# Two attention blocks on one core: the value sums of two groups of heads in one phase, and one buffer laid into another

## The chip, the cores and the metric

The kernel runs on one core of a Trainium2 chip. Its engines work side by side: TensorE (PE in the profile, with PEld for the loading of weights into its array), VectorE (DVE), ScalarE (ACT), GpSimd (POOL), and SyncE (SP), which here only issues DMAs. The metric is the time of one execution on the device in microseconds (us); smaller is better.

## The reference

Two independent blocks A and B, each with an input x of 2048 rows by 640, weights wqkv (640 x 1920) and wo (640 x 640), and 32 heads of 20 columns. Their outputs stand side by side in an output of 2048 x 1280.

```
A:  q, k, v = heads of x @ wqkv
    p = softmax(q k^T / sqrt(20)) over the keys 0 <= row - key < 256
    out = (p v) @ wo
B:  q, k, v = heads of x @ wqkv;  phi(t) = (t + 1 if t > 0 else exp(t)) + 1e-6
    kv = phi(k)^T v;  z = sum of phi(k);  o = phi(q) kv / (phi(q) z + 1e-6)
    out = o @ wo
```

## The kernel before

The rows are worked in 4 blocks s of 512. A's 32 heads are 8 groups g of 4 heads. All instructions of all engines are written in one order, and each engine works its own in that order; semaphores make one engine wait for another.

**Score tiles.** `scores` (L775) makes one tile: up to four heads' score products on PE into the only `S_ps` (4 of the 8 PSUM banks), one exponential on ACT of 128 x 2048 values into a buffer `p` (L805), and masks on POOL (`affine_select`, L826). There are 76 score tiles, numbered here 0 to 75: 16 in the first block, 20 in each other. `tiles_of` (L39) lists them: from the second block on, two groups g and h = g + 1 share five tiles. Tile 2 of the five completes nothing, tile 3 completes g, tile 5 completes h. Tiles 2 and 3 hold a middle part whose masks are larger (a 128 x 512 select and two of 128 x 1024 each); tiles 1, 4 and 5 have two selects of 128 x 512. In the first block two groups share four tiles, and the second and the fourth complete one each.

**Value sums.** `values` (L837) multiplies the p of one group with v: 56 matmuls (40 in the first block) that each use 32 columns of the array, four side by side, into one bank `dense`. For the group h its own order is: the middle part of tile 3, the parts of tile 4, the parts of tile 5. DVE then transposes the bank into `T` (L866, one buffer), and a deferred `rest` divides by the softmax sums (L877, L883). A group's sums are issued two tiles after the tile that completes it, straight behind that tile's score products.

**Fill.** All other PE work is fill: the projections of A and B, B's sums over keys, the output projections. It uses full 128 x 128 weights, and a chain of matmuls per bank (`dense`, 4 banks, shared with the value sums). A list `plan` gives every bank of fill a time in units of tiles, and other work (loads, DMA moves, selects) too; sorted by time it is one sequence. After each tile's products and value sums, `take` (L1101) issues fill until the tile's credit of matmul columns is used: `rate` columns per tile, less `VALUES` for each value sum. PSUM banks are copied out by ACT or DVE, whichever the counters of `evac` (L266) find less loaded; banks of phi take an exponential on ACT and two DVE operations (L301, L304), which are deferred in `later` until the next `flush`.

**Parts that the change touches.** A's v projection of a block (`a_v`, L469) reads v's weights `w_sb["A"]`; the last block's has plan times 43 to 49, its q 36 to 41.5 and its k 41 to 46. `kv_T` (L524) holds B's kv in blocks of 120 columns with zeros between; GpSimd clears it at the start (L525), `b_kv` (L640) has DVE copy the products into it (L656, L663), `own_heads` (L621) masks them with two POOL selects, and `b_merge` (L666) multiplies them with wo. `zk` is masked by two small POOL selects (L224). q's and k's rows for the groups 5 to 7 are moved by 4 DMA writes and 4 DMA reads through DRAM (`moves`, L379).

```
        if ready and ready[0][0] + LAG <= i:
            ...
            _, at = ready.popleft()
            values(*at, held.pop(at))
            ...
            credit -= VALUES
```

Of the kernel before, what the change touches and what calls it, by code (L numbers as in the profile page):

```python
# [9 lines left out]
P = 128  # L10
# [3 lines left out]
BF16 = mybir.dt.bfloat16  # L14
# [5 lines left out]
NG = H // 4  # L20
# [3 lines left out]
FILL = 386520  # L24
TAIL = 13000

VALUES = 2200
TILE = 3000
COPY = 160
AHEAD = 600  # L30
# [72 lines left out]
def kernel(  # L103
# [10 lines left out]
    nc = tc.nc  # L114
    _, S, D = A_x.shape
    KT = D // P
    NS = S // SB
# [7 lines left out]
    def pool(name, bufs, space=None):  # L125
        if space is None:
            return ctx.enter_context(tc.tile_pool(name=name, bufs=bufs))
        return ctx.enter_context(tc.tile_pool(name=name, bufs=bufs, space=space))

    wp = pool("weights", 1)  # L130
# [1 line left out]
    qp = pool("q", 2)  # L132
    kp = pool("k", 3)
    vp = pool("v", 3)
    pp = pool("p", 5)
    pqp = pool("pq", 2)
    op1 = pool("o1", 2)
    pl_ = pool("plow", 2)
# [11 lines left out]
    w_sb = {}  # L150
# [87 lines left out]
    def flush(before=None):  # L238

        while later and (before is None or later[0][0] <= before):  # L240
            later.pop(0)[1]()
# [90 lines left out]
    for c in range(KT):  # L332
        m = EXTRA * c
        while m < EXTRA * (c + 1):
            n = min(EXTRA * (c + 1) - m, DH - m % DH)
# [184 lines left out]
    GD = GH * DH  # L520
    NGR = KT + 1
    PAD = GD
    G = w_sb["B"][:, :, D : 2 * D]
    kv_T = wp.tile([P, NGR, PAD + GD + 8 * KT], BF16, name="kv_T")  # L524
    nc.gpsimd.memset(kv_T[:], 0.0)  # L525
    kv_own = kv_T[0:GD, :, PAD : PAD + GD]

    pk_of = {}
# [104 lines left out]
    def kv_ready(step):  # L633

        if step == 0:
            keep_own_head(zk[:], 0, NHC, 1)
        else:
            own_heads(3 - 2 * step)

    def b_kv():  # L640

        for gs in (range(0, 4), range(4, NGR)):
            ps = bank()
            for i, g in enumerate(gs):
                w = min(GD, D - g * GD)
                for kt in range(KT):
                    nc.tensor.matmul(  # L647
                        ps[0:w, i * GD : i * GD + w],
                        lhsT=w_sb["B"][:, kt, 2 * D + g * GD : 2 * D + g * GD + w],
                        rhs=G[:, kt, g * GD : g * GD + w],  # L650
                        start=(kt == 0),
                        stop=(kt == KT - 1),
                    )
                yield KT * GD
            full = [g for g in gs if (g + 1) * GD <= D]
            nc.vector.tensor_copy(  # L656
                out=kv_own[:, full[0] : full[-1] + 1, :],
                in_=ps[0:GD, 0 : len(full) * GD].rearrange("p (g d) -> p g d", d=GD),
            )
            if len(full) < len(gs):  # L660
                w = D - KT * GD
                at = len(full) * GD
                nc.vector.tensor_copy(out=kv_own[0:w, KT, 0:w], in_=ps[0:w, at : at + w])  # L663
            yield End(0)
# [107 lines left out]
    def key(s, rel):  # L772
        return 4 * s + rel
# [63 lines left out]
    def values(s, g, held):  # L837


        O_ps = dps.tile([P, SB], F32, name="dense")  # L840
        todo = []
        for (_, rel, q0, n, col, step), (p, low) in held:
            if rel == "M":
                own = key(s, q0 // P)
                todo.append((own, low, q0, n, col - LOW, step, columns))
                if own >= 2:
                    todo.append((own - 2, p, q0 + HALF, n, col, step, columns_p))
            else:
                todo.append((key(s, rel), p, q0, n, col, step, columns_p))
        for i, (kb, p, q0, n, col, step, of) in enumerate(todo):  # L850
            at = (kb % TPS * H + 4 * g) * HV
            for j in range(4):
                nc.tensor.matmul(  # L853
                    O_ps[32 * j : 32 * (j + 1), q0 : q0 + n],
                    lhsT=v_flat[kb // TPS % 3][:, at + j * HV : at + j * HV + 32],
                    rhs=of(p, j, col, n, step),
                    start=(i == 0),
                    stop=(i == len(todo) - 1),
                    tile_position=(0, 32 * j),
                    skip_group_check=True,  # L860
                )
        if turns[0] and g == 0:
            settle()

        T = tp.tile([P, SB // 32, 32], F32, name="T")
        nc.vector.transpose(out=T.rearrange("p b e -> p (b e)"), in_=O_ps[:])  # L866
        add_load(d=1500)
        if s not in norm_A:
            norm_A[s] = (
                np_.tile([P, SB // 32, P], BF16, name="N"),  # L870
                np_.tile([P, SB // 32, 32], BF16, name="Nr"),
            )
        N, Nr = norm_A[s]

        def rest():
            r = sp.tile([P, SB // 32, 1], F32, name="recA")
            nc.vector.reciprocal(out=r[:], in_=T[:, :, DH:HV])  # L877
            lo = g * DH
            for dst, a, b in ((N, lo, min(lo + DH, P)), (Nr, max(lo, P), lo + DH)):
                if a >= b:  # L880
                    continue
                at = a - P if dst is Nr else a
                nc.vector.tensor_tensor(  # L883
                    out=dst[:, :, at : at + b - a],
                    in0=T[:, :, a - lo : b - lo],
                    in1=r[:].to_broadcast([P, SB // 32, b - a]),
                    op=ALU.mult,
                )
            if lo < P <= lo + DH:
                oT_A[s] = op1.tile([P, KT, SB], BF16, name="oT")  # L890

                def turn(j):
                    quadrant = slice(32 * j, 32 * (j + 1))
                    nc.sync.dma_start_transpose(
                        out=oT_A[s][:, j, :].rearrange("p (b e) -> p b e", e=32),
                        in_=N[quadrant].rearrange("p b x -> p (b x)"),
                    )
                    turns[0] -= 1

                if s < NS - 1:  # L900
                    turns[0] = 4
                    for j in range(4):
                        soon(lambda j=j: turn(j), 2 + 2 * j)
            if g == NG - 1:
                nc.vector.transpose(
                    out=oT_A[s][:, KT - 1, :], in_=Nr.rearrange("p b e -> p (b e)")
                )

        later.append((begun[0], rest))
# [123 lines left out]
    def at(t0, t1, gen, n):  # L1033
        for i in range(n):
            plan.append((t0 + (i + 0.5) / n * (t1 - t0), gen, i == n - 1))

    def do(t0, t1, fns):
        fns = list(fns)
        for i, fn in enumerate(fns):
            plan.append((t0 + (i + 0.5) / len(fns) * (t1 - t0), None, fn))  # L1040
# [12 lines left out]
        at(t - 0.5, t + 3.5, first_rows[n], c)  # L1053
        reads_of(t + 5, t + 6, n, 0)
    for s, tq, tk, tv in ((1, (2.2, 8), (7, 12), (10, 15)), (2, (19, 26), (25, 32), (16, 22)),
                          (3, (36, 41.5), (41, 46), (43, 49))):
        at(*tq, a_rows("q", s), KT)
        reads_of(tq[1] + 1.5, tq[1] + 3.5, "q", s)
        at(*tk, a_rows("k", s), KT)
        reads_of(tk[1] + 1.5, tk[1] + 3.5, "k", s)  # L1060
        at(*tv, a_v(s), 2 * TPS)
# [4 lines left out]
    for s, t in ((0, 6), (1, 11), (2, 24.2), (3, 28.2)):  # L1066
        do(t, t, [lambda s=s: load_tok(s)])
    do(40.5, 40.5, [lambda: kv_ready(0)])
    at(42, 43.4, b_kv(), 2)
    do(44, 45.4, [lambda c=c: kv_ready(c) for c in (1, 2)])  # L1070
    for s, tq, td, tx in ((0, (39.5, 45), 46.3, 46.8), (1, (45, 50), 53, 54.3),
# [36 lines left out]
        return done  # L1108

    units = [u for s in range(NS) for u in tiles_of(s)]  # L1110
    LAG = 2
    held, ready = {}, deque()
    n_values = NS * NG
    rate = (FILL - TAIL + n_values * VALUES) / len(units)
    credit = 0.0
    for i, (s, parts, selects, done) in enumerate(units):
        p = scores(s, parts, selects)
        flush()
        credit += rate
        for part in parts:  # L1120
            held.setdefault((s, part[0]), []).append((part, p))
        if done is not None:
            ready.append((i, (s, done)))
        if ready and ready[0][0] + LAG <= i:
            last = i == len(units) - 1
            if last:
                credit -= take(2000)
            _, at = ready.popleft()
            values(*at, held.pop(at))
            if last:  # L1130
                flush()
            credit -= VALUES
            if len(quotients_due) > 2 or i > URGENT:
                quotient()
        else:
            quotient()
        credit -= take(credit)
        pass_tile()
    while ready:
        take(5500)  # L1140
        _, at = ready.popleft()
        values(*at, held.pop(at))
        flush()
    turn_last(NS - 1)
    for _ in fill:
        pass
# [31 lines left out]
```

## Time and profile before

| | |
|---|---|
| time, median of 3 runs | 255.71 us (255.31 to 256.76) |
| time of the profiled execution | 256.37 us |
| its span | 254.6 us |
| PE busy | 244.4 us |
| ACT, DVE, POOL busy | 199.2, 181.6, 170.7 us |
| stretch 180.6 to 238.1 us (last block's tiles): ACT, DVE, POOL busy of 57.5 us | 51.5, 50.0, 43.2 us |
| granted TensorE clock | 1.00 |

The span is the time from the first to the last instruction of the program; 1.77 us of the profiled execution lie around it. PE matmuls are pipelined: a row's length holds the latency of its last matmul, so the distance from one start to the next tells what a matmul costs, and the row's length does not. A row of the timeline that ends in [x <- y] had its engine idle for x us before it, and y is what ended the wait.

### The profile page before, as it was taken

What the parts mean: (1) busy time and instruction counts of PE and PEld (TensorE: products, weight loads), DVE (VectorE), ACT (ScalarE), POOL (GpSimd) and SP (SyncE); (2) the same over time, 40 slices, a digit from 0 to 9 for tenths busy, and PEclk for the clock granted to TensorE, in tenths of its full rate; (3) what the DMA queues carried; (4) which work ended last, traced back from release to release, by engine and by line L of the source; (5) the groups of instructions that cost most, each with busy time, mean ns of one, the idle gap of its engine ahead of it and who ended that gap; (6) DMA issues with size and microseconds to landing.
All of it is one profiled execution on the core that took longest, in us unless ns stands there. A gap on an engine that the chain in (4) does not pass through costs nothing.

```text
span 254.6 us, 10488 instructions
## 1 busy us (share of the span) xinstructions
PE 244.4 (96%) x4578; PEld 142.9 (56%) x4625; DVE 181.6 (71%) x315; ACT 199.2 (78%) x261; POOL 170.7 (67%) x214
## 2 busy tenths in 40 slices
PE   8999999999999999999999999999999999999995
PEld 7644446557755455466445555556555565655573
DVE  0445797697854578777665877688879889979652
ACT  3566879889768797997668788899988999998442
POOL 7115788778784957658495867959676695987700
PEclk9999999999999999999999999999999999999999
DMA  6996588798660342995468395525769987584714
GB/s 215 311 219 194 109 194 130 189 263 156 96 96 3 90 147 36 240 273 149 83 127 170 87 207 103 145 43 78 199 83 180 178 98 151 97 177 81 234 45 164
DMA packets 68371, 37.16 MB, mean 146 GB/s; under 512 B 51557, under 2 KB 67301, under 8 KB 68325
## 3 DMA queue, kind: packets, MB, share of 16 engines
q1 hardware_dynamic: 68325, 36.49, 66.2%
q8 instruction: 36, 0.59, 1.0%
q14 instruction: 10, 0.08, 0.1%
HBM read 14.42 MB, written 9.83 MB: 95 GB/s over the span
## 4 chain that ended last, share of the span: by engine, by line
PE 90%; issue 4%; DVE 4%; ACT 1%; ACTq 0%
PE dense L287 48%; PE S_ps L785 11%; PE dense L853 9%; PE dense L564 9%; PE dense L422 9%; PE dense L207 1%; DVE phi L304 1%; PE dense L718 1%; ACT e L297 1%; PE dense L188 1%; PE dense L675 1%; PE dense L647 1%; DVE tok L754 1%; DVE e L301 1%; ACT osb L272 0%
## 5 line engine op out<-in xcount | busy, mean ns | idle before, releaser
L805 ACT ACTIVATE p<-S_ps 128x2048 bf16<-128x2048 f32 x76 | 142.1, 1870 | 31.0 <-PE S_ps L785 30.4
L826 POOL TENSOR_SCALAR_AFFINE_SELECT p<-p 128x512 bf16<-128x512 bf16 (+1 forms) x152 | 121.7, 823 | 62.6 <-ACT p L805 60.3
L287 PE MATMUL dense<-xA,wqk 128*128 128x512 bf16 x188 | 48.9, 380 | 1.3 <-issue 0.8
L826 POOL TENSOR_SCALAR_AFFINE_SELECT plow<-p 128x1024 bf16<-128x1024 bf16 x32 | 40.4, 1261 | 0.0
L785 PEld LDWEIGHTS <-kpad 20*128 20x128 bf16 (+1 forms) x1664 | 20.0, 97 | 27.9 <-issue 26.5
L785 PE MATMUL S_ps<-qpad,kpad 20*128 20x64 bf16 (+3 forms) x1664 | 34.6, 211 | 1.0 <-issue 0.4
L866 DVE STREAM_TRANSPOSE T<-dense 128x512 f32<-128x512 f32 x32 | 22.7, 710 | 15.7 <-PE dense L853 15.3
L301 DVE TENSOR_SCALAR e<-e 128x512 bf16<-128x512 bf16 x40 | 23.6, 590 | 13.2 <-ACT e L297 13.0
L287 PEld LDWEIGHTS <-wqk 128*128 128x128 bf16 x200 | 17.9, 98 | 20.6 <-issue 2.3
L304 DVE SCALAR_TENSOR_TENSOR phi<-dense,e 128x512 bf16<-128x512 f32 x40 | 27.7, 691 | 1.6
L422 PE MATMUL dense<-wA,xA 128*128 128x320 bf16 x160 | 26.5, 303 | 0.2 <-issue 0.2
L853 PE MATMUL dense<-p,vA 128*32 128x64 bf16 (+2 forms) x1152 | 26.1, 222 | 0.1
L287 PE MATMUL dense<-wB,xB 128*128 128x512 bf16 (+1 forms) x156 | 25.3, 297 | 0.4 <-issue 0.3
L297 ACT ACTIVATE e<-dense 128x512 bf16<-128x512 f32 x40 | 23.4, 592 | 2.5 <-PE dense L287 1.9
L287 PE MATMUL dense<-wo,oT 128*128 128x128 bf16 (+2 forms) x155 | 24.5, 297 | 0.5 <-issue 0.2
L287 PE MATMUL dense<-xB,wB 128*128 128x512 bf16 x90 | 24.4, 380 | 0.5 <-issue 0.3
L564 PE MATMUL dense<-tok,phi 128*128 128x129 bf16 (+1 forms) x152 | 23.9, 296 | 0.9 <-issue 0.8
L287 PE MATMUL dense<-wB,xA 128*128 128x128 bf16 (+1 forms) x152 | 22.8, 295 | 0.7 <-issue 0.5
L853 PEld LDWEIGHTS <-vA 128*32 128x32 bf16 x1664 | 21.5, 96 | 3.3 <-issue 0.8
L883 DVE TENSOR_TENSOR N<-T,recA 128x320 bf16<-128x320 f32 (+1 forms) x28 | 19.6, 698 | 2.7 <-DMA oT<-N 1.8
L272 ACT ACTIVATE osb<-dense 128x512 bf16<-128x512 f32 (+1 forms) x26 | 14.6, 571 | 7.6 <-PE dense L287 7.1
L422 PEld LDWEIGHTS <-xA 128*128 128x128 bf16 x160 | 15.2, 99 | 8.0 <-issue 0.4
(66 smaller groups left out, 241.6 us busy)
## 6 DMA issues: line engine op xcount, KB each, us to landing
out_dram<-osb SPq DMA_DIRECT2D x7, 640.0 KB
x_scr<-xB SPq DMA_DIRECT2D x4, 640.0 KB
tok<-in_B_x_dram SPq DMA_DIRECT2D x4, 640.0 KB
xB<-x_scr SPq DMA_DIRECT2D x4, 640.0 KB
wB<-in_B_wqkv_dram SPq DMA_DIRECT2D x3, 800.0 KB
q_scr<-qpad SPq DMA_DIRECT2D x16, 60.0 KB
k_scr<-kpad SPq DMA_DIRECT2D x16, 60.0 KB
qpad<-q_scr SPq DMA_DIRECT2D x16, 60.0 KB
```

The costliest lines, as they stand in the source:

```text
L287: nc.tensor.matmul(dst, lhsT=lhs(kt), rhs=rhs(kt), start=(kt == 0), stop=(kt == KT - 1))
L297: nc.scalar.activation(out=view(e), in_=src, func=ACT.Exp)
L301: nc.vector.tensor_scalar(out=e[:], in0=e[:], scalar1=1e-6, scalar2=1.0 + 1e-6, op0=ALU.add, op1=ALU.min)
L304: nc.vector.scalar_tensor_tensor(out=dst, in0=src, scalar=0.0, in1=view(e), op0=ALU.max, op1=ALU.add)
L422: nc.tensor.matmul(ps[:, 0 : hh * DH], lhsT=xt[:, kt, tb * P : (tb + 1) * P], rhs=w_sb["A"][:, kt, i * hh * DH : (i + 1) * hh * DH], start ...
L564: nc.tensor.matmul(out, lhsT=pk[:, tb, c * P : (c + 1) * P], rhs=x[:, tb, lo:hi], start=(i == 0), stop=(i == len(blocks) - 1),)
L785: nc.tensor.matmul(columns(S_ps[0:keys], j, col, n, step), lhsT=kt[32 * j : 32 * j + DH, g, ko : ko + keys], rhs=q_pad[s][32 * j : 32 * j ...
L805: nc.scalar.activation(out=p.rearrange("p a j q -> p j a q"), in_=S_ps.rearrange("p j (a q) -> p j a q", a=2), func=ACT.Exp, scale=scale,)
L826: nc.gpsimd.affine_select(out=dst, in_=src, pattern=[[0, 4], [0, n // HALF], [sgn, HALF]], compare_op=ALU.is_ge, fill=0.0, base=base, chan ...
L853: nc.tensor.matmul(O_ps[32 * j : 32 * (j + 1), q0 : q0 + n], lhsT=v_flat[kb // TPS % 3][:, at + j * HV : at + j * HV + 32], rhs=of(p, j, c ...
L866: nc.vector.transpose(out=T.rearrange("p b e -> p (b e)"), in_=O_ps[:])
L883: nc.vector.tensor_tensor(out=dst[:, :, at : at + b - a], in0=T[:, :, a - lo : b - lo], in1=r[:].to_broadcast([P, SB // 32, b - a]), op=AL ...
```

## The change

- From now on the sums of both groups of a pair are issued in one phase, `values` twice in a row, g first. From the second block on this is one tile after tile 5 (before: g in tile 5 and h two tiles after tile 5). In the first block it is two tiles after the fourth tile. The last two groups of the last block stay as they were. Between the two, the first group's `rest` is flushed.
- `VALUES` goes from 2200 to 1500 columns, so that `rate` goes from 5841 to 5546 columns per tile.
- There are six p buffers, not five.
- `kv_T` is no tile of its own any more. It is the first 1680 columns of v's weights of A, and so it can be cleared only when A's last v projection is done: the clearing moves from the start to plan time 41, behind `zk`'s selects at 40.5.
- A's last v projection moves from 43..49 to 35.8..40.6, q from 36..41.5 to 38.5..44.5 and k from 41..46 to 43..48. Their DMA moves follow.

```
-VALUES = 2200
+VALUES = 1500
...
-    pp = pool("p", 5)
+    pp = pool("p", 6)
...
-    kv_T = wp.tile([P, NGR, PAD + GD + 8 * KT], BF16, name="kv_T")
-    nc.gpsimd.memset(kv_T[:], 0.0)
+
+    KVW = PAD + GD + 8 * KT
+    kv_T = w_sb["A"].rearrange("p k n -> p (k n)")[:, 0 : NGR * KVW].rearrange(
+        "p (g w) -> p g w", w=KVW
+    )
...
-                          (3, (36, 41.5), (41, 46), (43, 49))):
+                          (3, (38.5, 44.5), (43, 48), (35.8, 40.6))):
...
     do(40.5, 40.5, [lambda: kv_ready(0)])
+    do(41, 41, [lambda: nc.gpsimd.memset(kv_T, 0.0)])
     at(42, 43.4, b_kv(), 2)
...
-        if done is not None:
-            ready.append((i, (s, done)))
-        if ready and ready[0][0] + LAG <= i:
+
+        single = (s, done) in ((NS - 1, NG - 2), (NS - 1, NG - 1))
+        if done is not None and (done % 2 or single):
+            lag = 1 if s and not single else 2
+            ready.append((i + lag, s, (done,) if single else (done - 1, done)))
+        if ready and ready[0][0] <= i:
             last = i == len(units) - 1
             if last:
                 credit -= take(2000)
-            _, at = ready.popleft()
-            values(*at, held.pop(at))
-            if last:
-                flush()
-            credit -= VALUES
+            _, sv, groups = ready.popleft()
+            for g in groups:
+                values(sv, g, held.pop((sv, g)))
+                if last or g != groups[-1]:
+                    flush()
+                credit -= VALUES
             if len(quotients_due) > 2 or i > URGENT:
                 quotient()
         else:
...
     while ready:
         take(5500)
-        _, at = ready.popleft()
-        values(*at, held.pop(at))
-        flush()
+        _, sv, groups = ready.popleft()
+        for g in groups:
+            values(sv, g, held.pop((sv, g)))
+            flush()
```

## The prediction

> **What bounds the kernel now.** I read the page first: busy shares, the slices, the chain that ended last.
>
> ```profile
> PE 244.4 (96%) x4578; PEld 142.9 (56%) x4625; DVE 181.6 (71%) x315; ACT 199.2 (78%) x261; POOL 170.7 (67%) x214
> PE   8999999999999999999999999999999999999995
> PE 90%; issue 4%; DVE 4%; ACT 1%; ACTq 0%
> ```
>
> PE is full in every slice and carries the chain, so time goes only where PE is given less, or made to wait. The waits of PE in the list of waits are small (2.1 us on "issue" is the largest), so I next looked at what PE pays for a phase of value sums. The timeline of PE over tile 32, which has one, and tile 33, which has none:
>
> ```profile
> 109.57 0.55 PE L785 MATMUL S_ps<-qpad,kpad 20*128 20x192 bf16 x40
> 110.04 0.21 PE L853 MATMUL dense<-plow,vA 128*32 128x64 bf16 x4
> ...
> 110.26 0.66 PE L853 MATMUL dense<-p,vA 128*32 128x64 bf16 x28
> 110.84 1.25 PE L287 MATMUL dense<-wB,xB 128*128 128x512 bf16 x4
> ...
> 112.46 0.54 PE L785 MATMUL S_ps<-qpad,kpad 20*128 20x64 bf16 x40
> 112.94 0.60 PE L287 MATMUL dense<-xA,wqk 128*128 128x512 bf16 x2
> ```
>
> By the starts, scores and sums take 110.84 - 109.57 = 1.27 us and the same scores alone 0.48: the phase costs 0.79. Then POOL, because the change lets a pair's second sums follow their masks by one tile where there were two, and puts work into POOL's queue. Its timeline at tiles 42 to 46, the groups of kv's selects and clearing, and a late stretch:
>
> ```profile
> 141.21 0.69 POOL L826 TENSOR_SCALAR_AFFINE_SELECT p<-p 128x512 bf16<-128x512 bf16 x1 [0.39 <-ACT p L805]
> 141.85 1.39 POOL L826 TENSOR_SCALAR_AFFINE_SELECT plow<-p 128x1024 bf16<-128x1024 bf16 x1
> 143.31 1.15 POOL L826 TENSOR_SCALAR_AFFINE_SELECT p<-p 128x1024 bf16<-128x1024 bf16 x1
> 144.93 0.67 POOL L826 TENSOR_SCALAR_AFFINE_SELECT p<-p 128x512 bf16<-128x512 bf16 x1 [0.46 <-ACT p L805]
> ...
> 150.76 1.57 POOL L826 TENSOR_SCALAR_AFFINE_SELECT p<-p 128x512 bf16<-128x512 bf16 x2 [1.55 <-ACT p L805]
> ```
> ```profile
> L623 POOL TENSOR_SCALAR_AFFINE_SELECT kv_T<-kv_T 120x720 bf16<-120x720 bf16 x2 | 2.2, 1083 | 0.0
> L525 POOL MEMSET kv_T<- 128x1680 bf16 x1 | 1.5, 1497 | 0.0
> L224 POOL TENSOR_SCALAR_AFFINE_SELECT zk<-zk 128x40 bf16<-128x40 bf16 x2 | 1.1, 531 | 0.1
> ```
> ```profile
> 222.01 4.66 POOL L826 TENSOR_SCALAR_AFFINE_SELECT p<-p 128x1024 bf16<-128x1024 bf16 x5
> ```
>
> The reader is to see that POOL waits for ACT before tiles 42, 43 and 45: it has slack, but a tile of the large masks takes 3.1 us of a tile's 2.9. In the late stretch five selects run with no wait between them: no slack there.
>
> **The change part by part.** The sum is made against the profiled execution, 256.37 us (span 254.6 and 1.77 around it); the median of the runs is 0.66 less, and the forecast is put on the median.
>
> *Phases joined.* Of 32 phases, 15 vanish: four pairs in each of three blocks, three in the last. What is saved is what a phase costs beyond its matmuls. The matmuls of a phase hold 1536 columns; ten fill matmuls of 512 start 0.217 apart (210.65 to 212.82), so 1536 cost 0.65 at full rate, and 0.14 of 0.79 is left. Some of that is inside the phase: starts run from 110.04 to 110.66, and the last piece of 192 columns streams another 0.08, so the sums fill 0.70. That leaves 0.09 to 0.10 for the switch between the two uses of the array. I take 0.10: 15 x 0.10 = 1.5 us saved; ends 1.2 (0.08) and 2.1 (0.14). The Trainium skill, "TensorEngine Tiling (Array Packing)", section Key Properties, says that a change of tiling mode drains the array, and "TensorE: Matmul & The Clock Gate", section Single matmul latency, gives a constant of 398 cycles at 2.4 GHz, an estimated 0.17 for a drain; by it the saving would be 2.5. The 0.10 of the rows is taken.
>
> *Fill, VALUES, rate.* No column of fill comes or goes. Tiles without sums get 5546 columns (2.35 us), not 5841 (2.47); the pair's tile gets 2546 (1.1) beside two phases (1.4). From the rows: a tile of 40 products is 0.48 + 2.35 + 0.1 = 2.9 long, of 8 products 2.8, the pair's tile 0.33 + 1.42 + 0.1 + 1.1 = 2.95. The exponential ends 2.35 to 2.5 after the scores start (148.36 to 150.69 at tile 45), so the next scores find `S_ps` free with 0.3 to spare where ACT is not late. Nothing is taken; ends 0 and +0.8.
>
> *The first clearing of kv_T removed.* It ran from 3.70 to 5.20, and POOL then idled 5.2 until weights landed at 10.40: worth nothing.
>
> *The clearing at its new place.* I counted columns in plan order (2560 a bank of q, k or B, 1600 a bank of v) against credit. A's last v bank ends in tile 43's fill, and zk's two selects and the clearing go into POOL's queue behind tile 43's masks and ahead of tile 44's. With tile 42's scores at 0, the scores of 43, 44, 45, 46 start at 2.8, 5.7, 8.55, 11.5. POOL: masks of 42 from 2.55 to 5.75, of 43 to 8.75, zk (2 x 0.53) to 9.85, clearing (1.50) to 11.35, masks of 44 to 12.65, of 45 to 13.95. The pair's second phase starts 0.33 + 0.71 after the scores of tile 46 and reaches the parts of tile 45 another 0.46 later (0.24 for the middle, 0.21 for tile 4): 13.0. PE waits **0.95**; ends 0.4 and 1.6. Queued behind the clearing on DVE: kv's first copy (L656, 146.38 now), held 1.7 us till 11.35, and behind it q's copy, kv's second and the pair's transposes. Their banks are wanted at 11.85 and free by 12.05, inside the 0.95.
>
> *kv's masks (L623).* By the same count the first falls into tile 47 (now 154.78, in tile 47 too but at its head, behind two small masks) behind a large mask, the second into 48 as before. POOL from tile 47's exponential: 3.2 + 1.1 + 3.05 + 1.06 + 1.3 + 1.3 = 11.0, so masks are done 13.5 after the scores of 47; the second phase of tile 51 wants them at 11.45 + 1.50 = 12.95. **+0.5**; ends 0 and 1.0.
>
> *One tile of lag elsewhere.* After tile 5's exponential its masks take 1.3 to 1.6, and the phase wants them 1.5 after the next scores, which start 0.3 to 0.6 later: covered by 0.2 to 0.7 in the first three blocks. In the last, where masks run without a wait, they end late by about 0.1 at tile 66 and 0.4 at tile 71 (226.67 against 224.86 + 1.50 now). **+0.4**; ends 0 and 1.2.
>
> *Two transposes in one tile.* DVE gets 2 x (0.71 + 0.26 + 0.75) = 3.4 us of a pair at once. The second bank is held until 1.9 us after its last matmul, and a phi bank left open over the phase about 5 us after the first. Two of four banks are then late, but others serve: chains at 211.7 start while phi's L304 is still to run (212.04). 0; ends -0.3 and +1.5.
>
> *Waits that go.* Sums at tile 62 wait for a bank (0.27 at 199.29), those of tile 55 some 0.2. Two phases have moved away: **-0.3**; ends -0.6 and 0.
>
> *No cost.* A sixth p buffer: the pair's five and the next tile's. v reads x first at tile 35, loaded by tile 33. v's third token block writes where tiles up to 36 read; its banks come at 38. SP: q's four reads go from tiles 44 to 47 to 50 to 54, k's from 53 to 55 to 56 and 57; the rows are first read at tile 68, eleven tiles (30 us) later. A's wo loads (16 DMAs or so, 0.5 us each) start two tiles later, at 43, ahead of kv's q transposes; used from tile 48 on, 14 us away. Quotients come sooner, as more tiles have no sums: DVE work unchanged.
>
> Sum: -1.5 + 0.95 + 0.5 + 0.4 - 0.3 = +0.05: 256.4 for a profiled execution, **255.8 on the median**.
>
> **Rivals.**
> *Faster.* The three mask waits don't come, because PE reaches the phases later than counted or POOL is earlier: -1.5 - 0.3 gives 253.9. For it: each wait is a difference of sums of ten durations, and 0.5 shift in either undoes it. Against: the clearing's 1.5 us has no idle POOL time near it, as masks of tiles 42 and 43 fill POOL. By the drain rule the same case ends at 252.9; nothing in the rows speaks for it.
> *Slower: POOL late in every pair.* Should tile 5's masks end 0.25 after they are wanted in each of 11 pairs, that is 2.75 more: 258.5. It decides where masks end over 1.5 us after the next scores' start; rows say 1.35 to 1.6 less 0.45, so it takes another 0.4 in each tile. Speaking for it: L301 on DVE runs 0.28 to 1.24 and the select of 512 0.66 to 1.6 while both are busy. The Trainium skill, "SBUF — State Buffer", states that DVE and GpSimd share a port pair that one holds for a whole instruction; the spread agrees with it.
> *Slower: banks.* If the open phi bank is the next one due, a chain starts at about 3.3 after the first phase and the bank is free at 5.0: 1.7 in each of the pairs at 31, 46, 61, 66 where phi is open. Two of them give 3.4: 259.2. Against: the start at 211.7.
>
> **Numbers.** Forecast 0.5, faster 0.22, masks late 0.16, banks 0.12. Half a per cent, 1.3 us, is about what a measurement can tell from no change: faster 0.22; the forecast spreads past +1.3 by its upper ends sometimes, so same 0.48, slower 0.30. The range leaves out the far half of the bank case and a tenth below: 253.6 to 258.6; the forecast's own is 254.4 to 257.2.
>
> **What would show it.** Right: 17 phases of sums; two sums' starts 0.71 apart; PE waiting for POOL about 0.9 us in the second phase of tile 46, 0.5 in that of 51 and less in 66 and 71; L525 late in tile 45, L656 right behind. Wrong: no wait of PE for L826, or waits in most pairs; or PE waiting for L304 or L866 after the pairs at 31, 46, 61, 66.

## The result, and the profile after

The changed kernel takes 269.50 us, median of 6 runs (268.15 to 270.94), against 256.33 (255.31 to 257.31) for the kernel before in the same job: ratio 1.0516, 95% interval 1.0464 to 1.0568. That is 13.2 us slower where no change was forecast, and far outside the range. The profiled execution took 268.15 us, its span is 266.4. Of each kernel some executions run at a lower granted clock and take longer; the ranges hold them, and the ratios leave out those that are marked slow.

From `scores` on, every line number below is three higher than in the kernel before (L785 is L788, L853 is L856, L866 is L869, L883 is L886, L894 is L897); the clearing is L1072.

The page of the changed kernel: busy times, PE's slices and clock, the fetching of instructions (packets, MB, share of the DMA engines), the chain.

```profile
PE 250.7 (94%) x4625; PEld 143.0 (54%) x4625; DVE 179.4 (67%) x318; ACT 198.8 (75%) x258; POOL 170.1 (64%) x214
PE   8999999999999999699997978999799899999995
PEclk9999999999999999999999997999999999999999
q8 instruction: 36, 0.59, 0.9%
PE 76%; DVE 9%; DMA 4%; issue 4%; POOL 3%; ACT 3%; SPq 0%; DVEq 0%; ACTq 0%
```

No other engine became the bound: all are busy for as long as before or less. PE has holes where it had none, and its clock has a dent. The list of PE's waits names them (total us, times, longest). In the kernel before its largest entry on "issue" is made of many short waits, and only one of 0.4 us stands at `S_ps`; the changed kernel's largest entries follow (a wait of 1.1 us at the start, L207, is in both and left out):

```profile
PE dense L287 <- issue: 2.1, 13, 0.2
PE S_ps L785 <- issue: 0.4, 1, 0.4
```
```profile
PE S_ps L788 <- issue: 6.0, 3, 2.5
PE dense L422 <- DVE T L869: 1.8, 1, 1.8
PE dense L287 <- DVE T L869: 1.2, 1, 1.2
PE dense L287 <- DVE phi L304: 0.9, 2, 0.5
PE dense L721 <- DVE phi L304: 0.7, 1, 0.7
```

The largest entry is "issue": PE stood and nothing that the profile records held it. The timeline of PE over the end of tile 31, whose phase of a pair's sums runs from 106.34 to 107.87, and over tile 32, which starts at 109.05, shows the first of the three:

```profile
106.02 0.40 PE L788 MATMUL S_ps<-qpad,kpad 20*128 20x256 bf16 x8
106.34 0.51 PE L856 MATMUL dense<-p,vA 128*32 128x256 bf16 x16
...
107.24 0.70 PE L856 MATMUL dense<-p,vA 128*32 128x64 bf16 x28
107.87 1.04 PE L287 MATMUL dense<-wB,xB 128*128 128x512 bf16 x4
108.74 0.38 PE L287 MATMUL dense<-xA,wqk 128*128 128x512 bf16 x1
109.05 0.51 PE L788 MATMUL S_ps<-qpad,kpad 20*128 20x192 bf16 x36
112.04 0.22 PE L788 MATMUL S_ps<-qpad,kpad 20*65 20x64 bf16 x4 [2.48 <-issue]
```

PE stops inside the score products of one tile: 36 of 40 are issued, the last four come 2.5 us later. They write the buffer that the other 36 write, and no semaphore that the profile shows came late. The second stop, in the tile behind the pair's phase of tile 46, is the same picture and costs clock besides (PE from tile 47 on):

```profile
157.79 0.47 PE L788 MATMUL S_ps<-qpad,kpad 20*128 20x192 bf16 x31
160.81 0.25 PE L788 MATMUL S_ps<-qpad,kpad 20*65 20x64 bf16 x9 [2.54 <-issue]
160.99 1.86 PE L287 MATMUL dense<-xA,wqk 128*128 128x512 bf16 x6
162.64 2.34 PE L287 MATMUL dense<-xB,wB 128*128 128x512 bf16 x5
164.91 0.72 PE L788 MATMUL S_ps<-qpad,kpad 20*128 20x64 bf16 x40
```

The five matmuls from 162.64 on take 0.45 us each, six before them 0.28 (1.65 by the starts), where 0.217 is usual: PE ran at about half rate. The trace has the granted clock at 0.50 from 161.93 to 165.34, which is the dent in the clock's row. The Trainium skill, "TensorE: Matmul & The Clock Gate", section What's actually happening, says that PE's clock falls to half after an idle window of about 3.4 us that runs freely. The trace agrees with the halving; here 2.5 us of idle were enough in tile 47, and 2.5 us in tile 32 cost no clock (in two runs below, 32 later and turns, a stop of 2.2 and 2.3 us there did).

**What stops PE.** PE's instructions are numbered here in program order: weight loads, matmuls, and the few semaphore and drain instructions that the trace has on PE's weight-load row (24 in the whole kernel before). The stops in tiles 32, 47 and 62 come behind numbers 3776, 5569 and 7361, which are 192, 193 and 193 above a multiple of 256; the one small stop of the kernel before (0.66 us, tile 43) comes behind 5056, which is 192 above one. And q8 of the page moves 36 packets of 0.59 MB / 36 = 16.4 KB, one for 2 x 4625 / 36 = 257 PE instructions. So PE's instructions arrive in pieces of 256. In the trace the packet for tile 47 runs from 158.17 to 159.31, while PE already stands, and PE goes on 1.5 us after its end; in tile 32 the packet runs from 109.17 to 110.41, and PE goes on at 112.04. The piece that ended at the stop of tile 47 had begun at 155.10, so the packet of the next one started 3.1 us after that. The DMA queues from 155.1 to that start (158.1), and while the packet moved (158.1 to 159.4):

```profile
q1 hardware_dynamic: 1261, 0.59, 116.4%
```

```profile
q1 hardware_dynamic: 91, 0.02, 10.0%
q8 instruction: 1, 0.02, 5.5%
```

The kernel's own DMAs (q1) filled the 16 DMA engines (packets overlap, hence over 100%) until the packet started, and hardly used them from then on.

A tile's fill uses few instructions for its time (0.217 us a matmul), a phase of sums many: 56 matmuls with their loads, 112 instructions, in 0.7 us. Two phases with the scores ahead of and behind them use up the 256 instructions ahead of the stop in 2.63 us in tile 32, 2.95 in tile 47, 2.76 in tile 62. In the kernel before three pieces were used in 3.1 to 3.3 us, and behind one of them came its stop. The Trainium skill, "Runtime: NRT & Kernel Launch", section Instruction fetch mechanics, says that instructions come in blocks of 256 and the next is fetched while the present one runs, so that the cost of a boundary is mostly hidden. The trace agrees with the 256; it isn't hidden in tiles 32, 47 and 62.

**What else is late.** N holds A's normalised value sums of a block; its products (L886) write it, and four transposing DMAs, the *turns* (L897), read it into `oT`. In tile 42 PE stands 2.2 us between two fill matmuls. DVE over these microseconds, and SP's queue:

```profile
139.75 0.25 DVE L880 RECIPROCAL recA<-T 128x16 f32<-128x16 f32 x1
143.52 0.92 DVE L886 TENSOR_TENSOR N<-T,recA 128x320 bf16<-128x320 f32 x1 [3.52 <-DMA oT<-N]
144.54 0.72 DVE L869 STREAM_TRANSPOSE T<-dense 128x512 f32<-128x512 f32 x1
```
```profile
136.30 0.53 SPq L966 DMA_DIRECT2D xB<-x_scr  x1
136.89 1.22 SPq L897 DMA_TRANSPOSE oT<-N  x1
```

N has one buffer. The last turn of the second block of rows left SP at 136.89, right behind a 640 KB load of x, and the third block's first product waits for it until 143.5. Behind that product DVE has the transposes that free PE's banks. The same wait was there before the change, in DVE's timeline then, with half the length and nobody behind it who was wanted:

```profile
137.57 0.49 DVE L883 TENSOR_TENSOR N<-T,recA 128x320 bf16<-128x320 f32 x1 [1.79 <-DMA oT<-N]
```

In tile 57 PE stands 1.3 us. DVE there shows the pair's second transpose behind the first sum's reciprocal and two products:

```profile
190.14 0.71 DVE L869 STREAM_TRANSPOSE T<-dense 128x512 f32<-128x512 f32 x1
190.88 0.25 DVE L880 RECIPROCAL recA<-T 128x16 f32<-128x16 f32 x1
191.17 0.29 DVE L886 TENSOR_TENSOR N<-T,recA 128x128 bf16<-128x128 f32 x1
191.38 0.81 DVE L886 TENSOR_TENSOR Nr<-T,recA 128x192 bf16<-128x192 f32 x1
192.29 0.72 DVE L869 STREAM_TRANSPOSE T<-dense 128x512 f32<-128x512 f32 x1
```

`T` has one buffer, so `rest` of the first sum must come between the two transposes, and the second bank stays held for 1.4 us longer than it need.

### The profile page after: what moved, and what is told of

Read it like the earlier page. It is cut to its first block, busy times and chain, and to the rows that moved or that the text cites. A ratio compares the mean times of both kernels' runs of the same rounds, so it can differ in the third digit from the quotient of the medians.

```text
span 266.4 us, 10539 instructions
## 1 busy us (share of the span) xinstructions
PE 250.7 (94%) x4625; PEld 143.0 (54%) x4625; DVE 179.4 (67%) x318; ACT 198.8 (75%) x258; POOL 170.1 (64%) x214
## 4 chain that ended last, share of the span: by engine, by line
PE 76%; DVE 9%; DMA 4%; issue 4%; POOL 3%; ACT 3%; SPq 0%; DVEq 0%; ACTq 0%
PE dense L287 41%; PE S_ps L788 9%; PE dense L567 9%; PE dense L422 8%; PE dense L856 6%; DMA oT<-N 2%; ACT p L808 2%; DVE tok L757 2%; DVE e L301 2%; POOL p L829 2%; DVE phi L304 2%; DMA out_dram<-osb 2%; DVE T L869 1%; PE dense L207 1%; DVE N L886 1%
## 5 line engine op out<-in xcount | busy, mean ns | idle before, releaser
L287 PE MATMUL dense<-xA,wqk 128*128 128x512 bf16 x200 | 50.6, 382 | 0.5 <-DVE phi L304 0.5
L788 PE MATMUL S_ps<-qpad,kpad 20*128 20x64 bf16 (+3 forms) x1664 | 35.1, 211 | 6.0 <-issue 6.0
L788 PEld LDWEIGHTS <-kpad 20*128 20x128 bf16 (+1 forms) x1664 | 20.4, 98 | 34.5 <-issue 33.2
L301 DVE TENSOR_SCALAR e<-e 128x512 bf16<-128x512 bf16 x40 | 20.0, 501 | 20.4 <-ACT e L297 20.3
L869 DVE STREAM_TRANSPOSE T<-dense 128x512 f32<-128x512 f32 x32 | 22.8, 713 | 9.7 <-PE dense L856 8.0
L287 PE MATMUL dense<-xB,wB 128*128 128x512 bf16 x100 | 27.0, 393 | 0.4 <-DVE osb L274 0.4
L287 PE MATMUL dense<-wB,xB 128*128 128x512 bf16 (+1 forms) x160 | 26.1, 300 | 0.0
L287 PE MATMUL dense<-wo,oT 128*128 128x512 bf16 (+2 forms) x160 | 24.8, 299 | 1.2 <-DVE T L869 1.2
L567 PE MATMUL dense<-tok,phi 128*128 128x129 bf16 (+1 forms) x160 | 25.7, 300 | 0.0
L287 PE MATMUL dense<-wB,xA 128*128 128x512 bf16 (+1 forms) x160 | 24.4, 299 | 0.3 <-DVE phi L304 0.3
L856 PE MATMUL dense<-p,vA 128*32 128x64 bf16 (+2 forms) x1152 | 24.6, 223 | 0.1
L856 PEld LDWEIGHTS <-vA 128*32 128x32 bf16 x1664 | 21.6, 96 | 3.5 <-issue 2.1
L886 DVE TENSOR_TENSOR N<-T,recA 128x320 bf16<-128x320 f32 (+1 forms) x28 | 17.5, 624 | 4.4 <-DMA oT<-N 3.5
L757 DVE TENSOR_TENSOR tok<-tok,rden 128x640 bf16<-128x640 bf16 x16 | 19.6, 1238 | 0.0
```

Of the source, the lines that this page charges most:

```text
L287: nc.tensor.matmul(dst, lhsT=lhs(kt), rhs=rhs(kt), start=(kt == 0), stop=(kt == KT - 1))
L301: nc.vector.tensor_scalar(out=e[:], in0=e[:], scalar1=1e-6, scalar2=1.0 + 1e-6, op0=ALU.add, op1=ALU.min)
L567: nc.tensor.matmul(out, lhsT=pk[:, tb, c * P : (c + 1) * P], rhs=x[:, tb, lo:hi], start=(i == 0), stop=(i == len(blocks) - 1),)
L757: nc.vector.tensor_tensor(out=vh, in0=vh, in1=rden_of[s][:, tb, :, :].to_broadcast([P, H, DH]), op=ALU.mult)
L788: nc.tensor.matmul(columns(S_ps[0:keys], j, col, n, step), lhsT=kt[32 * j : 32 * j + DH, g, ko : ko + keys], rhs=q_pad[s][32 * j : 32 * j ...
L856: nc.tensor.matmul(O_ps[32 * j : 32 * (j + 1), q0 : q0 + n], lhsT=v_flat[kb // TPS % 3][:, at + j * HV : at + j * HV + 32], rhs=of(p, j, c ...
```

## The experiments

Two theories at the outset: the loss is PE's instruction supply, which only the joined phases overload; or it is waits that the rest of the change makes (v ahead, kv's rows in the weights). Warm-up matmuls ahead of everything serve as a lever on the first: fewer of them, with more columns each, move every later instruction to an earlier place in its piece of 256 and change little else. Stops named below are distances over 0.53 us between two weight loads of PE, and a tile's length is that from its first score product to the next tile's.

**1. The change without its joined phases.**

```
-VALUES = 1500
+VALUES = 2200
...
-            lag = 1 if s and not single else 2
-            ready.append((i + lag, s, (done,) if single else (done - 1, done)))
+            ready.append((i, (s, done)))
...
+            values(*at, held.pop(at))
```

> The change without its joined phases: kv_T in v's weights, A's last v first and six p buffers stay, but the sums are issued one group at a time, two tiles after the tile that completes it, and VALUES is 2200 again. Theory F (instruction fetch): the big stalls belong to two phases in a row, so they go, and the time is that of the kernel before give or take 0.5 (255.5 to 257.5); no wait of PE on issue above 0.8 us. Theory R (the rest of the change: the clearing of kv_T, q and k late): most of the 13 us stays, 263 to 269.

Measured: 263.03 us (261.77 to 269.23), ratio 1.0232 (1.0150 to 1.0315), against 256.72 before in that job. Neither theory holds alone: the loss has two halves, some 6 us come without any joined phase, and joining adds about 7 (by the ratios). Tiles 0 to 34 are as in the kernel before to 0.05 us each; then PE stops 1.90 in tile 42, 1.17 and 1.15 in tile 45 (which is 4.50 us long, tile 46 is 3.02), 1.46 in 72 (and twice about 0.6). Tile 42 is the product behind the turn again. Tile 45 is the clearing, by DVE's and POOL's timelines of this run:

```profile
151.80 0.66 DVE L659 CAST wA<-dense 120x480 bf16<-120x480 f32 x1 [4.01 <-POOL wA L1072]
```
```profile
149.24 1.08 POOL L224 TENSOR_SCALAR_AFFINE_SELECT zk<-zk 128x40 bf16<-128x40 bf16 x2
150.27 1.50 POOL L1072 MEMSET wA<- 128x1680 bf16 x1
```

DVE stood four microseconds in front of kv's copy, and kv's second chain on PE (L650) and phi's banks stood behind DVE. In the changed kernel the same copy waited 1.18 us only: PE had already stood for 4.9 us in tiles 32 and 42, in which POOL caught up.

**2. and 3. The changed kernel, 32 PE instructions earlier and 32 later.** 12 warm-up matmuls of 288 columns, and 44 of 80, for 28 of 128.

```
-    dummies = warm_up((28, 3))
+    dummies = warm_up((12, 3))
```

> The changed kernel with 12 warm-up matmuls of 288 columns in the place of 28 of 128: the same columns ahead of the first real work, but every later PE instruction stands 32 places earlier. Theory F: PE gets its instructions in pieces of 256, and a piece that is used up in under 3 us is not followed in time. The places where a piece begins move, and by the counts of the changed kernel's trace no piece now ends in the tiles 32, 47 and 62 as early as before: the least time between the demand for a piece and its use goes from 3.3 to 4.8 us. The three stalls of 2.7, 2.7 and 1.2 us and the half clock behind the second go: 260 to 263. Theory B (banks and DMA waits of DVE behind the joined sums): nothing of that depends on the number of warm-up matmuls, 268 to 270.5 and the same three stalls in the same tiles.

> The changed kernel with 44 warm-up matmuls of 80 columns in the place of 28 of 128: later PE instructions stand 32 places later, and the first real work starts up to 1.7 us later. Theory F: the stalls move: one of 1.5 to 2.7 us in tile 18, behind the joined sums of tile 17, and less or nothing in 32, 47 and 62; 262 to 268. Theory B: 268 to 272 with the stalls in 32, 47 and 62.

Measured: 260.11 us (258.95 to 261.32), ratio 1.0119 (1.0055 to 1.0184), for the earlier place; 266.49 (265.44 to 269.90), ratio 1.0353 (1.0288 to 1.0419), for the later. Sixteen warm-up matmuls less are worth 9.4 us. PE over tile 32 with the earlier place:

```profile
108.85 0.55 PE L788 MATMUL S_ps<-qpad,kpad 20*128 20x192 bf16 x40
109.33 1.04 PE L287 MATMUL dense<-xA,wqk 128*128 128x512 bf16 x4
```

All 40 products go out together. The stops of tiles 32 and 62 and the half clock are gone, and with them the stops of tiles 69 and 70; in tile 47 there is one of 1.29 us left, behind the same number 5569, now between two fill matmuls. The run with the later place is a miss in part: the stop expected in tile 18 came (0.63), but those of tiles 32, 47 and 62 stayed (2.20, 2.53, 1.83). There I had reckoned with the time from 64 instructions ahead of a boundary; the whole piece ahead of the stop was still used in 2.75, 3.06 and 2.86 us. What the miss gave instead is the clearest sign of the pieces: the program stands 32 instructions later, and the stops are at the same numbers as without the shift. (Its profiled execution, 269.9 us, is the longest of its four, so the places of its stops are read more surely than their sizes.)

**4. The changed kernel with the turns given out at the next bank.**

```
-                        soon(lambda j=j: turn(j), 2 + 2 * j)
+                        soon(lambda j=j: turn(j), 1)
```

> The changed kernel with the four transposing DMAs of a block's first four oT chunks issued at the next bank, in the place of 2, 4, 6 and 8 banks later. In the changed kernel DVE waits 3.5 us at 140.0 for the last of them before it may write N again, and PE 1.8 to 2.0 us in tile 42 for a bank behind that. If that DMA's place in the queue is the cause, both waits go: 266.5 to 268.5. If the DMA is late for another reason, the time stays at 268.5 to 270.5.

Measured: 267.50 us (266.05 to 268.80), ratio 1.0405 (1.0341 to 1.0469). SP's queue has the four turns in one row, done 9 us before the product (143.24 in this run):

```profile
129.09 5.18 SPq L897 DMA_TRANSPOSE oT<-N  x4
```

Tile 42 goes from 4.80 to 2.80 us, and the product there waits for no DMA any more: that is the gain. The stops for instructions stay.

**5. Both, and the lever on the kernel before.**

> The changed kernel with two edits at once: 12 warm-up matmuls of 288 columns in the place of 28 of 128 (32 PE instructions fewer ahead of everything), and A's turn DMAs given out at the next bank rather than 2, 4, 6 and 8 banks later. If the lost time is two separate things, instruction pieces that arrive late and a normalisation queued behind a turn, the two gains add: 260.1 less the 2.0 that the turns alone brought, 257.5 to 259, with tile 42 at 2.8 to 3.0 us in the place of 4.25. If the turns' gain was only a stall that the pieces cause in another place, it stays at 259.5 to 261.

> The kernel before with the warm-up of 12 matmuls of 288 columns, nothing else. It tells whether fewer warm-up matmuls are worth something by themselves. Theory of the late instruction pieces: the kernel before has one such stall, 0.66 us in tile 43, which goes or moves; its other pieces last over 3.1 us; so 255.5 to 257 us, no more than 0.7 under the kernel before. Rival, that the shorter warm-up itself speeds every kernel that has it (by clock or by an earlier start): 248 to 253 us, as the 9 us that it brought to the changed kernel.

Measured: both together 257.49 us (257.19 to 259.51), ratio 1.0052 (1.0027 to 1.0078): the gains add (260.1 less 2.0, and 0.6 more). The kernel before with the short warm-up: 256.29 us (255.51 to 257.30), ratio 0.9986 (0.9966 to 1.0006). A short warm-up is worth nothing by itself; in that run the stop of tile 43 is gone (3.61 to 2.97 us) and another tile (28) is 0.35 longer.

**6. The change without joined phases, clearing on DVE, turns at the next bank.**

```
-    do(41, 41, [lambda: nc.gpsimd.memset(kv_T, 0.0)])
+    do(41, 41, [lambda: nc.vector.memset(kv_T, 0.0)])
```

> The change without its joined phases (263.0 us, 6 over the kernel before), with the clearing of kv's rows on DVE in the place of POOL, and A's turn DMAs at the next bank. Theory that its 6 us are waits behind the clearing (tiles 45 and 46: 1.17 and 1.15) and behind the turns (tile 42: 1.90): it falls by 3.5 to 4.5 us to 258.5 to 259.5, with tiles 42, 45 and 46 at about 3.0 us; the rest (tiles 56, 58, 72) stays. Rival, that the new order of v, q and k itself costs the time (the banks of q and k crowd tiles 43 to 49): it stays above 261.

Measured: 257.65 us (256.42 to 259.02), ratio 1.0039 (1.0010 to 1.0068), against 263.03. Tiles 42 and 45 fall from 4.50 and 4.50 to 2.74 and 2.72. More than expected, and all of the first half's loss but 1.2 us; what stops are left stand in tiles 56, 58 and 72 (0.56, 1.00, 1.70).

**7. The kernel before with v ahead alone.**

```
-                          (3, (36, 41.5), (41, 46), (43, 49))):
+                          (3, (38.5, 44.5), (43, 48), (35.8, 40.6))):
```

> The kernel before with one part of the change alone: A's last v ahead of its last q and k (no joined phases, kv's rows of their own, five p buffers). Theory that the 1.90 us which tile 42 lost without the joined phases come from this order (v's evictions and reads in the tiles where the second strip's normalisation is turned, so that a product stands behind a turn DMA and v's next bank behind the product): tile 42 at 4.3 to 4.7 us, 257.5 to 259. Rival, that they come from the sixth p buffer or from kv's rows in the weights: 255.8 to 256.8, with tile 42 at about 3.1.

Measured: 261.43 us (259.68 to 262.95), ratio 1.0204 (1.0134 to 1.0273). The theory's stop is there, 1.92 us in tile 42, with neither the sixth buffer nor kv's rows in the weights. (N's product waits 4.10 us there, and the eviction that PE waits for stands behind it; the profile names nothing that ended the product's wait, so that it was the turn is read from the run with the turns moved.) The size of the whole was missed by 2.4 us: the stop costs clock too (granted 0.50 from 142.03 to 145.45), and with the shift of the banks come stops for instructions. PE in this run:

```profile
141.68 0.21 PE L853 MATMUL dense<-plow,vA 128*32 128x64 bf16 x4 [1.71 <-DVE qpad L274]
...
142.85 2.31 PE L287 MATMUL dense<-xA,wqk 128*128 128x512 bf16 x5
```

Five matmuls in 2.1 us (142.85 to 144.96), where 1.1 is usual; tile 42 is 6.14 us long. The stops for instructions are 1.64 in tile 47 and 0.90 in tile 58 ("issue" in the list of waits).

**8. The joined phases repaired.** On top of run 5: clearing on DVE and a second `T` buffer, so that no `flush` stands between a pair's sums (three e buffers become two and two den one, for room). Then the second sum's `rest` given out one tile later. Then 8 warm-up matmuls of 432 columns, and 7 of 494.

```
-    tp = pool("turned", 1)
+    tp = pool("turned", 2)
...
-                if last or g != groups[-1]:
+                if last:
                     flush()
...
+            if len(groups) == 2:
+                put_off.append(later.pop())
```

> The changed kernel with the two edits of the run with both (12 warm-up matmuls of 288, turns at the next bank), the clearing on DVE, and a second T buffer, so that the turn of a pair's second sum no longer stands behind the first sum's reciprocal and products on DVE (room for it: two e buffers in the place of three, one den in the place of two). Theory of waits behind DVE's order: the 1.32 us of tile 57 go (PE waited there for the second turn, which stood behind 1.35 us of the first sum's reciprocal and products), so 1.3 to 2 us under the run with both: 256 to 257.5. Rival, that the banks were held for another reason, or that two e buffers hold phi back: the same or slower, 257.5 to 260.

> The run with two T buffers, and of each pair the second sum's reciprocal and products are given out one tile later than the first's, so that DVE doesn't get 2.9 us of them in a row. Theory that what is left of the joined phases' loss stands behind these products (tile 7: phi behind two products, 0.80; tile 74: an eviction behind two quotients that came late, 1.28): tile 7 at 2.7 to 2.9 us, 255.5 to 257, below the run with two T buffers (257.4) by 0.5 to 2. Rival, that a product given out later makes another tile late by as much: the same as the run with two T buffers, 257 to 258.

> The run before this one with 8 warm-up matmuls of 432 columns in the place of 12 of 288, which is 8 PE instructions fewer. Theory of the late instruction pieces: the 1.20 us at the boundary in tile 47 go, since the piece that ends there then starts earlier against the pair's phase; 1.0 to 1.3 us below that run: 254.3 to 256. Rival, that tile 47's stall is a bank's or a weight's wait: no change against that run.

> The run with 8 warm-up matmuls of 432 columns, with 7 of 494: two PE instructions fewer again. There every stall over 0.53 us behind the first tile was gone, and the tiles 0 to 75 took 217.2 us against 218.9 of the kernel before. Theory that nothing of the loss is left then and that the joined phases' drains are the gain: 1.0 to 1.7 us below the kernel before, ratio 0.993 to 0.997, the same tiles. Rival, that the gain there was chance: ratio 0.998 to 1.002.

| run | us, median | ratio to before | tiles that moved |
|---|---|---|---|
| two T buffers | 257.36 (256.34 to 258.18) | 1.0022 (1.0001 to 1.0043) | 57: 4.33 to 3.02, 58: 3.58 to 3.03; new stops in 47 (1.20) and 74 (1.28) |
| and `rest` put off | 256.40 (255.29 to 257.13) | 1.0001 (0.9977 to 1.0024) | 7: 3.48 to 2.90, 74: 3.65 to 2.59 |
| and 8 instructions fewer | 255.80 (254.62 to 256.95) | 0.9977 (0.9951 to 1.0002) | 47: 4.34 to 2.96 |
| and 2 fewer again | 255.52 (254.99 to 257.56) | 0.9970 (0.9945 to 0.9995) | 48: 2.96 to 3.66 |

The first gained 0.1 where 1.3 to 2 were expected: tile 57 was mended as foreseen, and a stop for instructions and two quotients on DVE took the gain back elsewhere. The other three came within their ranges or at the edge: 8 instructions fewer gained 0.6 where 1.0 to 1.3 were expected, and the last row 0.9 where 1.0 to 1.7 were, with a new stop of 0.71 us in tile 48. The stop that eight instructions remove, PE in tile 47 with `rest` put off, and then with the 8 fewer:

```profile
154.77 0.38 PE L287 MATMUL dense<-xB,wB 128*128 128x512 bf16 x1
156.37 1.02 PE L287 MATMUL dense<-xB,wB 128*128 128x512 bf16 x4 [1.22 <-issue]
```
```profile
154.27 1.24 PE L287 MATMUL dense<-xB,wB 128*128 128x512 bf16 x5
155.44 0.54 PE L788 MATMUL S_ps<-qpad,kpad 20*128 20x64 bf16 x40
```

With the 8 fewer no stop over 0.53 us is left from tile 0 on, and PE's row of slices is full again:

```profile
PE   8999999999999999999999999999999999999995
PE 81%; DVE 7%; POOL 4%; ACT 3%; DMA 2%; issue 2%; SPq 0%; DVEq 0%; ACTq 0%
```

The last row of the table is the one version that beat the kernel before by more than its interval: 255.52 against 256.43 us. That is a third of a per cent, the interval ends at 0.9995, and it is one of four versions, so the rival of chance (0.998 to 1.002) isn't excluded.

**Where the stops for instructions fall.** All stops of all runs, from tile 0 on and at full clock, in which PE waited for nothing that the profile shows, by number in program order:

| run | behind number (above a multiple of 256) | 256 instructions ahead of it used in, us | stop, us |
|---|---|---|---|
| kernel before | 5056 (192) | 3.29 | 0.66 |
| changed kernel | 3776 (192), 5569 (193), 7361 (193) | 2.63, 2.95, 2.76 | 2.68, 2.76, 1.23 |
| 32 earlier | 5569 (193) | 4.27 | 1.29 |
| 32 later | 2241 (193), 3776 (192), 5569 (193), 7361 (193) | 3.12, 2.75, 3.06, 2.86 | 0.63, 2.20, 2.53, 1.83 |
| turns at the next bank | 3776 (192), 5569 (193), 7361 (193) | 2.63, 3.00, 2.76 | 2.30, 1.66, 1.73 |
| without joined phases: run 1; run 6 | 6848 (192); 6848 (192) | 3.19; 3.19 | 0.66; 1.00 |
| v ahead alone | 5568 (192), 6848 (192) | 5.72, 3.19 | 1.64, 0.90 |
| run 5, both edits | 5057 (193) | 5.05 | 0.60 |
| run 8, four versions | 5569 (193) in three, none with 8 fewer | 4.04, 4.08, 5.28 | 1.20, 1.60, 0.71 |

Whatever the code there is (scores, sums, fill), the stop comes behind the instruction 192 or 193 above a multiple of 256, in all twenty. Fourteen of them follow a piece used in under 3.3 us. The other six follow one of 4.0 to 5.7 us, five of them at the same boundary 5569, so the speed of use alone doesn't decide.

The second thing is when the packet starts. In all fourteen traces (490 packets) the packets start in step with PE's crossing of these places, from 1.9 us before one to 5.4 us after it, and PE never crossed the next place sooner than 2.2 us after that packet's start and 1.2 us after its end. The stops end 2.2 to 2.9 us after the start (4.2 once, where the packet itself took 2.8) and 1.2 to 1.6 after the end. So PE stops where the packet's delay behind the crossing and these two to three microseconds are together more than the piece lasts; in the six slow cases the packet started 2.7 to 4.7 us after the crossing. The delay goes with the load on the DMA engines in the 1.5 us ahead of the packet: where they were under 60% busy, 1 packet of 264 started over 2 us after the crossing, and where they were 95% busy or more, 85 of 154 did. They were full ahead of the packets of 18 of the 20 stops; the exceptions are the kernel before (58%) and tile 18 of the run with 32 later (idle). No run moved the kernel's DMAs and left the instructions where they were, so that these DMAs hold the packets up is an association and was not tried.

**The sum.** From tile 0's scores to tile 75's the kernel before takes 218.90 us, the changed one 230.66, the version with 8 instructions fewer 217.19. The 13.5 us between the last two, by tiles:

| cause | tiles | us | shown by run |
|---|---|---|---|
| instructions late, with the half clock | 32; 47 and 48; 62 | 2.66 + 4.33 + 1.21 = 8.2 | 2, 8 |
| banks late after them | 69, 70 | 1.3 | 2 |
| product behind the turn | 42 | 2.0 | 4 |
| products ahead of the second transpose and of phi | 7; 57, 58 | 0.7 + 1.9 = 2.6 | 8 |
| the other tiles | | -0.6 | |

## Why the prediction was wrong

**Phases joined: right.** The joined phase of tile 31 is 1.53 us long (106.34 to 107.87) against 2 x 0.80 before, and over all clean phases 1.525 against 2 x 0.806; in the first block 1.127 against 2 x 0.621. That is 0.09 and 0.115 saved a time, 11 x 0.087 + 4 x 0.115 = 1.4 us of the 1.5 forecast. The estimate of 0.17 for a drain, from the Trainium skill's latency constant, was too high by half or more: the rows decide. In the version with 8 instructions fewer the tiles 0 to 75 take 1.7 us less than before, of which 0.66 is the stop that the kernel before had itself; so 1.0 of the 1.4 is left.

**Fill, VALUES, rate: the step that failed.** It asked whether PE, ACT and `S_ps` could keep the tile's new rhythm, and by durations they can. It put the term at nothing without asking whether PE gets its instructions in time. A pair's tile packs scores, two phases, five fill matmuls and the next scores, 16 + 224 + 10 + 80 = 330 instructions, into 3.4 us. The instruction supply was left out, not mis-sized: 8.2 us here, and 1.3 of banks late behind it, of some 13. The prediction named "issue" as the largest wait of PE and asked no further; 0.4 us of it stood at `S_ps`, where score products stopped halfway.

**No cost: wrong at SP's list.** It checked v's reads, the moves and the loads, but not the turns of N, whose place is counted in banks and which share SP's queue with all that moved. The new order of v, q and k alone is enough for a stop of 1.9 us in tile 42 (run 7). The wait of DVE for it, 1.79 us, was in the profile before.

**The clearing, kv's masks, one tile of lag: the mechanism right, the sizes not.** POOL did what was counted: zk, then the clearing, between the masks of tiles 43 and 44. A pair's phase that waits for the last masks shows it at the 106th of its 112 matmuls, where tile 5's parts begin, as a longer distance between two weight loads (0.03 us elsewhere). In the changed kernel that is 0.34 us in tile 46 and nothing in 51, 66 and 71. But POOL had caught up in PE's holes there, so run 5, which has the clearing on POOL and few holes, is the better trial: 0.25 in tile 46 (0.95 forecast), nothing in 51 (0.5), 0.28 in 71 (0.4 for 66 and 71). With the clearing on DVE and 8 instructions fewer it is 0.36 in 51 alone. Some 0.5 us in all against 1.85: differences of sums of ten durations, each taken on the late side. Without the joined phases the clearing cost 2.3 us of stops (run 1; tile 45 is 1.7 us longer for them), by the copy of kv that held DVE up and not by masks: "their banks are wanted at 11.85 and free by 12.05" is what fell there.

**Two transposes in one tile:** taken as 0, ends -0.3 and +1.5. It was +2.6 (tiles 7, 57, 58), beyond its upper end. The durations were right (0.72, 0.25, 0.8); but stops followed two of the fifteen pairs, one of them in the first block, where I had not looked: there it is a phi behind the second product (tile 7), and in tile 57 a bank behind the first.

**Waits that go:** of the right size. Tile 62 is 3.24 us long before and 2.96 in the runs in which it has no stop. But the row at 199.29 names ACT (L779) as what ended the 0.27, not a bank. And in the rival of late masks, "the select of 512 0.66 to 1.6" is a misreading: one such select lasts 0.66 to 1.24 in that trace, and the row of 1.57 holds two.

**The rivals.** None was it. "Banks" was nearest: its mechanism came at tiles 7, 57 and 58, and of the places 31, 46, 61 and 66 where it was put only at 66, where the second sum starts 0.3 to 0.4 us late. Whether DVE and POOL share a port here, as the prediction cites, no run tells apart.

## What to carry to other kernels

Where a phase is made of very short instructions, count them: in this kernel most stops for instructions followed 256 of them used in under 3.3 us, and 18 of 20 came where the kernel's own DMAs had filled the DMA engines. An "issue" wait in the middle of a run of like matmuls is the sign, and moving the whole program by a few instructions the cheapest test: a stop of this kind keeps its place in the count while the code moves. A reordering of work in time must be followed through every queue that counts its place in banks or tiles, and a buffer with a single copy, however cheap its operation, decides what stands behind it on its engine.

## What the hardware showed that was not expected

- A packet of 256 PE instructions (16.4 KB) took 0.9 to 1.7 us to move in the two kernels' traces (2.8 at most in the other runs), and in the changed kernel's stops PE went on 1.5 to 1.6 us after its end, 2.6 to 2.9 after its start. In tile 66 of that kernel 256 instructions were used in 2.70 us with no stop behind them: the packet of the next ones had started 3.5 us before the first of them was used. Packets that started over 2 us late did so, with few exceptions, while the kernel's own DMAs filled the 16 engines; that these hold the packets up was not tried.
- The same kernel ran in 269.5 or 260.1 us with 28 or 12 warm-up matmuls, and the kernel before in 256.4 or 256.3. What a change is worth can so depend on where its instructions fall, by up to 3.5% here.
- A change of use of the array, from 128 x 32 to 128 x 128 and back, costs about 0.1 us.
